# Casting loads on GpSimd for the weights and the first batches of an attention and gMLP kernel

## The chip, the cores and the metric

The kernel runs on one core of one Trainium2 chip. A core has five instruction queues that run side by side: TensorE (PE, matrix products; its weight loads are shown as PEld), VectorE (DVE), ScalarE (ACT), GpSimd (POOL) and SyncE (SP), which here only starts transfers. Sixteen DMA engines move the data between the memory of the chip (HBM) and the core's SBUF. Each queue works its own list strictly in order; semaphores tie the lists together.

The metric is the device time of one execution in microseconds (us). A run below is one timed execution; the profiled execution is another one.

## The reference

Sliding-window causal attention (window 64) over q, k, v of shape 8 batches x 8 heads x 576 positions x 64, all float32, then a gated MLP with a spatial product over the 576 positions.

```python
def _attn_ref(q, k, v):
    scores = (1 / np.sqrt(D)) * np.matmul(q, k.transpose(0, 1, 3, 2))
    rel = pos[:, None] - pos[None, :]
    scores = np.where((rel >= 0) & (rel < 64), scores, -1e9)
    attn = np.exp(scores - np.max(scores, axis=-1, keepdims=True))
    attn = attn / (np.sum(attn, axis=-1, keepdims=True) + 1e-09)
    return np.matmul(attn, v)

def _moe_ref(x, w_in, w_spatial, b_spatial, w_out):      # x: 8 x 576 x 512
    h = np.maximum(x @ w_in, 0.0)                        # w_in: 512 x 1024
    u, v = h[..., :512], h[..., 512:]
    v_n = (v - mean(v)) / np.sqrt(var(v) + 1e-06)
    v_s = np.einsum('ts,bsd->btd', w_spatial, v_n) + b_spatial[None, :, None]
    return (u * v_s) @ w_out                             # w_out: 512 x 512
```

## The kernel before

All products run in float16; inputs and output are float32. The work is cut into named steps. A step is one or a few instructions of one engine, and the string ORDER (line 18) lists all of them with their engine and the number of the buffer or PSUM bank that they take. The kernel walks that list and emits the steps, so each engine's queue is the list filtered for that engine; there is no loop that could reorder anything. `DQ` is SP's queue of transfers. `PH` is a TensorE step whose matmuls are issued as two halves of 64 columns of the weights.

The names, with batch b, half g of the heads (four heads each) and further digits:

- `D`: 27 warm-up steps of TensorE on a scratch tile (line 862), 25 with two matmuls of 512 columns, D25 and D26 with nine of 128.
- `ldk`, `ldq` (line 412): one transfer of 128 rows x 4608 B in float32 into a buffer of the tag `nat`; `ck`, `cq`: cast to float16 into `hqk` (helper `cp`, lines 290 to 300; on GpSimd in three pieces); `tk`, `tq` (line 419): 32 x 32 block transposes on VectorE.
- `ldv` (line 433): five transfers per b and g, 128 positions x 4 heads x 256 B each (the last one 64 positions), into `natv`; `cv`: casts into `hv`; `sl`, `su`, `s4`: copies between the partition halves into `hs`, the values shifted by 64 positions.
- `S` scores on TensorE (line 479, into a pair of PSUM banks), `E` exponential on ScalarE (486), `M` mask by a minimum on VectorE (489), `Z` row sums by a product with ones (502), `N` and `n` logarithm and negative exponential on ScalarE (529, 531) for the reciprocal, `P` the product with the values (514), `X` the product with the reciprocal on VectorE (522). `S_r` to `X_r` do the last 64 positions.
- `V` and `U` are the two halves of x @ w_in, `Vr` and `Ur` their ReLU on ScalarE (669, 763), `Vb`, `Va` the statistics on VectorE (671, 673), `L1`, `L2` the reciprocal root on ScalarE (716, 718), `A` the normalization (728), `G` the spatial product, `Ge` the gate (797), `O` the output product, `Oe` its copy, `st` the store.
- `ldwin`, `ldwsp`, `ldb`, `ldwo` load the weights in float32 into `nat` buffers; `cwin`, `cwsp`, `cb`, `cwo` cast them. `W` transposes w_spatial on TensorE (378), `We` copies it out of PSUM.

A batch's G steps need A of all five row groups and all We; its U and V steps need the cast w_in and X. Eight `nat` buffers are shared by q, k and the weights. Batches overlap: while the gMLP part of batch b runs, the attention part of b+1 and the loads of later ones are in flight.

The opening of the order before, as the engines see it: TensorE has ten D steps, then S0_0, six D, S0_r, and the first G step (G0_0) after V0, U0, W, Z1_10, Z1_11 and Z1_r. VectorE starts with the mask copies (lines 252 to 258), then ck0_0, tk0_0, cq0_0, tq0_0, tk0_1, cq0_1, tq0_1. GpSimd builds `keep`, the identity and the ones rows first (lines 244 to 264) and then has casts and half copies only. SP starts with ldb, ldk0_0, ldq0_0, ldk0_1, ldv0_00, ldq0_1.

Of the kernel before, what the change touches and what calls it, by code (L numbers as in the profile page):

```python
# [11 lines left out]
ALU = mybir.AluOpType  # L12
# [27 lines left out]
cq2_0:POOL:0 M1_10:DVE ldv1_10:DQ:3 Ur0_2:ACT:0 L10:ACT:0 ldv1_11:DQ ldv1_12:DQ ldv1_13:DQ L20:ACT  # L40
ldv1_14:DQ ldq2_1:DQ:5 ldv1_04:DQ ldk2_1:DQ:6 ldwo00:DQ:0 ldwo01:DQ Ur0_4:ACT:1 S1_r:PE:0:1
Z1_10:PE:3 U0_0:PE:1 ldwo10:DQ:7 ldwo11:DQ U0_1:PE:2 E1_r0:ACT:0 Ur0_3:ACT:2 E1_r1:ACT Ur0_0:ACT:3
N1_10:ACT:3 A0_0:DVE:0 A0_3:DVE:1 cwsp4:DVE Ur0_1:ACT:4 W1:PE:0 W3:PE:1 W2:PE:3 W0:PE:2 A0_1:DVE:2
A0_4:DVE M1_11:DVE We1:DVE M1_r:DVE n1_00:ACT We2:ACT We3:ACT A0_2:DVE:3 We0:DVE W4:PE:0 ldq3_0:DQ:1
ldk3_0:DQ:2 ldv2_00:DQ:1 ck2_0:POOL:2 We4:DVE D17:PE:3 Z1_11:PE:1 Z1_r:PE:2 G0_0:PH:3 G0_1:PH:0
tq2_0:DVE:2 n1_10:ACT N1_11:ACT:0 tk2_0:DVE:3 Ge0_0:DVE:0 cv1_00:ACT:2 n1_01:ACT sl1_00:POOL:2
n1_11:ACT su1_00:ACT N1_r:ACT:2 cv1_01:POOL Ge0_1:DVE:1 su1_01:DVE G0_3:PH:1 sl1_01:POOL
cv1_10:ACT:3 Ge0_3:DVE:2 cv1_11:DVE S2_0:PE:0:1 P1_01:PE:2 P1_00:PE:3 X1_00:DVE:2 G0_2:PH:0
sl1_10:POOL:3 ldv2_01:DQ ldv2_02:DQ su1_10:ACT sl1_11:ACT E2_01:ACT:3 n1_r:ACT su1_11:POOL
s41_1:POOL P1_10:PE:1 X1_01:DVE P1_11:PE:3 G0_4:PE:2 X1_10:DVE:3 X1_11:DVE U1_1:PH:1 cq2_1:POOL:3  # L50
E2_00:ACT:2 M2_01:DVE Ur1_1:ACT:5 Ge0_4:DVE:3 ck2_1:POOL:1 ldv2_03:DQ V1_2:PH:3 cwo01:POOL
cwo10:POOL cwo11:POOL Ge0_2:DVE:4 M2_00:DVE Z2_01:PE:2 s41_0:ACT Vr1_2:ACT:5 N2_01:ACT:1 U1_2:PH:1
Ur1_2:ACT:3 P1_r:PE:0 V1_1:PH:3 Vr1_1:ACT:6 cq3_0:POOL:0 Z2_00:PE:2 V1_3:PE:1 tq2_1:DVE:4
Vb1_2:DVE:5 V1_0:PE:3 ck3_0:POOL:2 tk2_1:DVE:5 S2_1:PE:1:0 X1_r:DVE:1 N2_00:ACT:4 Vr1_3:ACT:7
cwo00:ACT V1_4:PE:2 Vr1_0:ACT:1 U1_4:PH:1 O0_2:PH:0 Vb1_1:DVE:2 Vb1_3:DVE:3 Vb1_0:DVE:1 ldv2_10:DQ:0
E2_10:ACT:0 Vr1_4:ACT:2 ldv2_11:DQ Va1_3:DVE M2_10:DVE U1_3:PH:3 E2_11:ACT:1 cv2_00:POOL:0
Ur1_4:ACT:4 Va1_0:DVE Vb1_4:DVE:0 M2_11:DVE Va1_4:DVE Va1_2:DVE Va1_1:DVE Z2_10:PE:1 S2_r:PE:1:0
Oe0_2:ACT:0 Oe0_4:ACT:0 ldv2_12:DQ ldv2_13:DQ ldv2_14:DQ E2_r0:ACT:0 N2_10:ACT:5 ldk3_1:DQ:3
ldq3_1:DQ:4 ldk4_0:DQ:5 U1_0:PE:0 O0_3:PE:2 O0_0:PE:1 ldv3_10:DQ:3 ldv2_04:DQ tq3_0:DVE:7 E2_r1:ACT
L11:ACT:1 Ur1_0:ACT:2 Ur1_3:ACT:1 L21:ACT ldv3_11:DQ O0_1:PE:0 M2_r:DVE tk3_0:DVE:8 S3_0:PE:1:0  # L60
n2_00:ACT Oe0_3:ACT Oe0_0:ACT:1 A1_0:DVE:4 A1_1:DVE:5 A1_2:DVE:6 A1_3:DVE:7 A1_4:DVE sl2_00:ACT:0
Oe0_1:ACT Z2_r:PE:3 Z2_11:PE:2 N2_11:ACT:3 su2_00:DVE cv2_10:DVE:1 sl2_10:POOL:1 N2_r:ACT:0
ldv3_12:DQ st0_4:DQ ldv3_13:DQ G1_3:PH:1 G1_4:PH:0 P2_00:PE:2 P2_01:PE:3 s42_1:POOL su2_10:POOL
# [137 lines left out]
def kernel(  # L201
# [57 lines left out]
    NSB = 2  # L259
    mv_t = [cpool.tile([128, 5, 2], f32, name=f"mv{i}") for i in range(NSB)]  # L260
    vn4_t = [cpool.tile([65, 512], f16, name=f"vn4_{i}") for i in range(NSB)]
    for i in range(NSB):
        nc.vector.memset(mv_t[i][:], 1.0)
        nc.gpsimd.memset(vn4_t[i][64:65, :], 1.0)
# [37 lines left out]
    def cost(n, a=True, d=True, p=True, d1=False):  # L302
# [8 lines left out]
        return out  # L311

    WIN, WSP, WOUT = {}, [], []

    def win_steps(key):
# [600 lines left out]
```

## Time and profile before

| what | us |
|---|---|
| median of three runs | 196.23 |
| lowest and highest run | 195.93, 197.76 |
| span of the profiled execution | 193.6 |
| PE busy in the span | 184.9 |
| DVE busy | 163.7 |
| ACT busy | 157.1 |
| POOL busy | 87.4 |

The span runs from the first to the last instruction of the profiled execution; what lies around it (start and end of the program) isn't in it. For the profiled execution only its span is given; the median of the runs is 2.6 us longer than that. Busy time of PE counts overlapping matmuls once, and the warm-up steps too. The page's other figures that matter: DMA queues moved 42.73 MB at a mean of 221 GB/s, 50421 packets, 39377 of them under 512 B (the pieces of v). All transfers but three small groups start on SP's queue, none on GpSimd's.

In the rows that follow, a row of the timeline is start, duration, engine, line, operation, output <- input, count, and in brackets the idle time before it with what ended it.

### The profile page before, as it was taken

How to read it: one execution, taken by the hardware profiler on the slowest of the kernel's cores; microseconds unless marked ns; L12 is line 12 of the kernel's file. 1: busy time of each engine (PE TensorE's matmuls, PEld its weight loads, DVE VectorE, ACT ScalarE, POOL GpSimd, SP SyncE). 2: the span in 40 equal slices, each digit the busy share in tenths (PEclk: the TensorE clock that was granted, in tenths of full speed). 3: DMA queues.
4: the chain of work that ended last, by engine and by line, in shares of the span. 5: the costliest groups of instructions: out<-in, count | busy, mean ns of one | idle time of the engine just before them, and what ended most of it. 6: DMA issues, size and time to landing. Idle time of an engine off the chain costs nothing.

```text
span 193.6 us, 7606 instructions
## 1 busy us (share of the span) xinstructions
PE 184.9 (95%) x3218; PEld 107.0 (55%) x3218; DVE 163.7 (85%) x304; ACT 157.1 (81%) x282; POOL 87.4 (45%) x161
## 2 busy tenths in 40 slices
PE   7798998999999999999999999999999999999991
PEld 2352534556556664656665656565756565665560
DVE  4899899999999999998999999998996967468331
ACT  2269998998999999899979999999999875706430
POOL 4027775849932986701956577615641520000000
PEclk9999999999999999999999999999999999999999
DMA  5999999899989997619987999669958000600445
GB/s 177 373 316 290 391 355 333 168 275 373 242 205 332 261 335 179 149 38 289 367 230 184 310 310 282 196 177 218 306 125 266 22 3 0 224 30 0 135 166 191
DMA packets 50421, 42.73 MB, mean 221 GB/s; under 512 B 39377, under 2 KB 39761, under 8 KB 50386
## 3 DMA queue, kind: packets, MB, share of 16 engines
q1 hardware_dynamic: 50162, 42.04, 73.3%
q8 instruction: 25, 0.41, 0.9%
q10 hardware_dynamic: 224, 0.20, 0.3%
q14 instruction: 10, 0.08, 0.1%
HBM read 32.79 MB, written 9.44 MB: 218 GB/s over the span
## 4 chain that ended last, share of the span: by engine, by line
PE 70%; DVE 13%; ACT 9%; DMA 3%; issue 2%; SPq 1%
PE bank L617 50%; PE bank L614 4%; PE pair L479 4%; PE bank L514 3%; DMA nk<-in_k_dram 3%; PE bank L502 3%; ACT e L486 3%; DVE qT L419 2%; PE bank L702 2%; DVE e L489 2%; DVE kT L419 2%; DVE st L671 2%; DVE g L797 1%; DVE x L522 1%; ACT lz L529 1%
## 5 line engine op out<-in xcount | busy, mean ns | idle before, releaser
L617 PE MATMUL bank<-wspT,vn 128*64 128x512 f16 (+3 forms) x530 | 39.1, 296 | 0.0
L486 ACT ACTIVATE e<-pair 128x1024 f16<-128x1024 f32 x32 | 32.0, 1030 | 1.6 <-PE pair L479 1.4
L797 DVE TENSOR_TENSOR g<-bank,ru 128x512 f16<-128x512 f32 (+1 forms) x36 | 23.3, 654 | 9.4 <-PE bank L617 7.0
L647 ACT COPY ob<-bank 128x512 f32<-128x512 f32 (+1 forms) x38 | 21.9, 591 | 9.7 <-PE bank L617 8.4
L669 ACT ACTIVATE vs<-bank 128x512 f16<-128x512 f32 (+1 forms) x40 | 23.8, 602 | 7.1 <-PE bank L705 5.6
L617 PE MATMUL bank<-x,win 128*64 128x512 f16 (+2 forms) x304 | 29.1, 327 | 0.0
L617 PEld LDWEIGHTS <-vn 128*64 128x64 f16 (+1 forms) x530 | 20.8, 111 | 13.2 <-issue 0.2
L671 DVE BATCH_NORM_STATS2 st<-vs 128x6 f32<-128x512 f16 (+1 forms) x40 | 26.0, 670 | 2.3 <-ACT vs L669 2.2
L298 POOL COPY hs<-hv 64x512 f16<-64x512 f16 (+1 forms) x36 | 20.1, 585 | 16.3 <-ACT hv L292 8.4
L617 PE MATMUL bank<-win,x 128*64 128x512 f16 x216 | 27.0, 379 | 0.0
L617 PE MATMUL bank<-wout,g 128*64 128x512 f16 (+1 forms) x208 | 24.7, 371 | 0.0
L522 DVE TENSOR_TENSOR x<-bank,lz 128x512 f16<-128x512 f32 x32 | 21.2, 684 | 3.5 <-PE bank L514 2.2
L489 DVE TENSOR_TENSOR e<-e,mask 128x1024 f16<-128x1024 f16 x32 | 23.0, 725 | 0.5 <-ACT e L486 0.4
L763 ACT ACTIVATE ru<-bank 128x512 f32<-128x512 f32 (+1 forms) x38 | 21.6, 584 | 1.5 <-PE bank L617 0.8
L295 POOL CAST hk<-nk 128x384 f16<-128x384 f32 x36 | 19.4, 574 | 7.1 <-DMA nk<-in_k_dram 6.7
L529 ACT ACTIVATE lz<-bank 128x512 f32<-128x512 f32 x32 | 19.0, 599 | 1.9 <-PE bank L502 1.6
L298 POOL CAST hv<-nv 128x512 f16<-128x512 f32 x18 | 11.7, 661 | 18.8 <-DMA nv<-in_v_dram 18.7
L419 DVE STREAM_TRANSPOSE kT<-hk 128x576 f32<-128x576 f32 x16 | 19.9, 1241 | 0.2 <-ACT hk L292 0.2
L419 DVE STREAM_TRANSPOSE qT<-hq 128x576 f32<-128x576 f32 x16 | 19.8, 1237 | 0.2
L531 ACT ACTIVATE lz<-lz 128x512 f32<-128x512 f32 x32 | 19.6, 642 | 0.0
L295 POOL CAST hq<-nq 128x384 f16<-128x384 f32 x27 | 14.9, 588 | 10.3 <-DMA nq<-in_q_dram 7.8
L617 PEld LDWEIGHTS <-win 128*64 128x64 f16 x304 | 14.4, 110 | 9.2
(91 smaller groups left out, 298.9 us busy)
## 6 DMA issues: line engine op xcount, KB each, us to landing
nk<-in_k_dram SPq DMA_DIRECT2D x16, 576.0 KB, 6.6
nq<-in_q_dram SPq DMA_DIRECT2D x16, 576.0 KB, 6.1
nv<-in_v_dram SPq DMA_DIRECT2D x64, 128.0 KB, 5.9
out_dram<-ob SPq DMA_DIRECT2D x14, 512.0 KB, 5.8
wi<-in_moe_w_in_dram SPq DMA_DIRECT2D x8, 256.0 KB, 5.8
ws<-in_moe_w_spatial_dram SPq DMA_DIRECT2D x4, 288.0 KB, 7.6
nv<-in_v_dram SPq DMA_DIRECT2D x16, 64.0 KB, 4.5
wo<-in_moe_w_out_dram SPq DMA_DIRECT2D x4, 256.0 KB, 7.2
```

The source lines that it names most:

```text
L295: nc.gpsimd.tensor_copy(o[:, n:n + 384], i[:, n:n + 384])
L298: nc.gpsimd.tensor_copy(o[:, lo:hi, :, :], i[:, lo:hi, :, :])
L419: d = add(f"t{name}{b}_{g}", ("DVE", 1.09), key, lambda e: nc.vector.transpose(qt.t[:, :].rearrange("p (i j) -> p j i", j=18), h.t[:, :].b ...
L486: ex = add(f"E{b}_{g}{u}", ("ACT", 0.91), key, lambda e, u=u: nc.scalar.activation(e2[u].t[:, :, :], sc[u].t[:, :, :], AF.Exp, bias=0.0, s ...
L489: mins.append(add(f"M{b}_{g}{u}", ("DVE", 0.65), key, lambda e, u=u: nc.vector.tensor_tensor(e2[u].t[:, :, :], e2[u].t[:, :, :], mask[:, : ...
L522: lambda e, u=u, ob=ob, lz=lz: nc.vector.tensor_tensor(x.t[:, u, :], ob.t[:, :], lz.t[:, :], ALU.mult),
L617: nc.tensor.matmul(o[c:c + 64, :], w[:, c:c + 64], x, start=start, stop=stop)
L647: lambda e: (nc.vector.tensor_copy if last else nc.scalar.copy)(view(), m.t[rows, 0:n]),
L669: rl = add(f"Vr{b}_{j}", ("ACT", 0.49), key, lambda e: nc.scalar.activation(vs.t[0:jn, :], m.t[0:jn, :], AF.Relu), deps=[pv], acq=[vs], us ...
L671: s1 = add(f"Vb{b}_{j}", ("DVE", 0.6), key + 0.02, lambda e: nc.vector.bn_stats(st6.t[0:jn, 0:6], vs.t[0:jn, :]), deps=[rl], acq=[st6], us ...
L763: lambda e, m=m, ru=ru, n=n: nc.scalar.activation(ru.t[:, 0:n], m.t[:, 0:n], AF.Relu), deps=[pu], acq=[ru], uses=[m])))
L797: nc.vector.tensor_tensor(g.t[:, 0:n], m.t[:, 0:n], ru.t[:, 0:n], ALU.mult)
```

## The change

Weights, q, k and v of batches 0 and 1, and q and k of batch 2 are now loaded by transfers that GpSimd starts and that turn float32 into float16 on the way. Their casts on VectorE, ScalarE and GpSimd are gone. The destinations are the same `nat` buffers (seen as float16), `hv` for v, and the weight tiles themselves, which become one tile each so that one transfer fills four row groups. w_spatial goes to a `nat` buffer and its last 64 rows to `ob4`. `keep`, the mask copies and the constants become steps of the order (`keep`, `mask`, `consts`), behind the first transfers. A step `hold` on GpSimd reads the last such q or k buffer and writes one element of the buffer of q of batch 3; the load ldq3_0, now the first of SP's queue, depends on it. From batch 2's v on, the loads are as before. The order is written anew; the opening is shown to the first G step.

```diff
 ORDER = """
...
+ldk0_0:POOL:0 ldk0_1:POOL:1 ldq0_0:POOL:2 keep:POOL mask:DVE D24:PE:0 D5:PE:1 D21:PE:2 D18:PE:3
+ldq0_1:POOL:3 ldv0_00:POOL:0 ldq1_0:POOL:4 ldv0_04:POOL ldv0_01:POOL consts:POOL D2:PE:0
+ldv0_10:POOL:1 ldv0_14:POOL ldv0_11:POOL D14:PE:1 D19:PE:2 D10:PE:3 D3:PE:0 ldk1_0:POOL:5 D1:PE:1
+D22:PE:2 D15:PE:3 ldwin1:POOL D6:PE:0 D0:PE:1 tk0_0:DVE:0 D26:PE:2 tq0_0:DVE:1 S0_0:PE:0:1
+E0_01:ACT:0 ldwsp4:POOL:0 ldk1_1:POOL:6 ldq1_1:POOL:7 tk0_1:DVE:2 D23:PE:3 ldwsp0:POOL:0
+ldwin0:POOL tq0_1:DVE:3 E0_00:ACT:1 S0_r:PE:1:0 D8:PE:0 M0_00:DVE D16:PE:1 ldb:POOL ldv1_10:POOL:2
+ldv1_11:POOL E0_r0:ACT:0 sl0_00:ACT:0 su0_00:DVE s40_0:DVE E0_r1:ACT S0_1:PE:1:0 M0_r:DVE
+E0_10:ACT:2 Z0_r:PE:2 N0_r:ACT:0 M0_01:DVE Z0_00:PE:3 D7:PE:0 N0_00:ACT:1 tq1_0:DVE:4 Z0_01:PE:1
+D4:PE:0 N0_01:ACT:2 n0_01:ACT ldq2_0:POOL:2 ldk2_0:POOL:1 M0_10:DVE sl0_01:DVE su0_01:DVE D12:PE:2
+D20:PE:3 D11:PE:0 ldv1_00:POOL:3 P0_00:PE:1 D25:PE:2 ldv1_01:POOL sl1_10:POOL:1 ldq2_1:POOL:3
+ldk2_1:POOL:4 ldwo:POOL su1_11:POOL su1_10:POOL sl0_10:DVE:2 s40_1:DVE su0_10:DVE sl0_11:DVE
+su0_11:DVE E0_11:ACT:3 M0_11:DVE n0_00:ACT X0_00:DVE:0 Z0_10:PE:3 Z0_11:PE:0 N0_10:ACT:3
+sl1_11:POOL n0_10:ACT N0_11:ACT:4 n0_r:ACT n0_11:ACT tk1_0:DVE:5 D13:PE:2 P0_01:PE:3 P0_10:PE:1
+X0_10:DVE:1 P0_r:PE:2 X0_r:DVE:0 S1_0:PE:1:0 X0_01:DVE P0_11:PE:0 X0_11:DVE E1_00:ACT:1 M1_00:DVE
+E1_01:ACT:0 M1_01:DVE V0_4:PE:1 Vr0_4:ACT:0 Vb0_4:DVE:0 V0_3:PE:2 Z1_00:PE:3 Vr0_3:ACT:1
+N1_00:ACT:5 sl1_00:POOL:3 su1_00:POOL V0_1:PH:0 Vr0_1:ACT:2 tk1_1:DVE:6 Z1_01:PE:1 tq1_1:DVE:7
+V0_2:PE:2 sl1_01:POOL ldv1_04:POOL Vr0_2:ACT:3 Vb0_2:DVE:1 Va0_2:DVE Vb0_1:DVE:2 hold:POOL:5
+V0_0:PE:3 Vr0_0:ACT:4 Va0_4:DVE ldv1_14:POOL Va0_1:DVE ldq3_0:DQ ldv2_10:DQ:0 ldv2_13:DQ
+ldv2_00:DQ:1 ldv2_01:DQ ldk3_0:DQ:6 ldv2_02:DQ ldv2_03:DQ ldv2_11:DQ ldv2_12:DQ S1_1:PE:1:0
+E1_10:ACT:2 s41_0:POOL D9:PE:0 E1_11:ACT:3 W2:PE:2 W3:PE:3 We2:DVE D17:PE:0 Vb0_0:DVE:3 W4:PE:2
+W0:PE:0 Va0_0:DVE M1_10:DVE Vb0_3:DVE:4 Va0_3:DVE We4:ACT N1_01:ACT:1 S1_r:PE:1:0 We3:DVE L10:ACT:0
+L20:ACT A0_3:DVE:0 A0_1:DVE:1 We0:ACT W1:PE:2 U0_0:PE:1 U0_2:PE:3 We1:ACT n1_01:ACT A0_4:DVE
+U0_4:PE:0 U0_3:PE:2 Ur0_0:ACT:0 Ur0_2:ACT:1 Ur0_4:ACT:2 cq3_0:POOL:0 ck3_0:POOL:1 Ur0_3:ACT:3
+E1_r0:ACT:0 M1_11:DVE A0_0:DVE:2 A0_2:DVE:3 G0_4:PH:1 Ge0_4:DVE:0 Z1_10:PE:3 N1_10:ACT:3 E1_r1:ACT
...
-    w_in_sb = [cpool.tile([128, 1024], f16, name=f"win{r}") for r in range(4)]
-    w_out_sb = [cpool.tile([128, 512], f16, name=f"wout{r}") for r in range(4)]
+    w_in_all = cpool.tile([128, 4, 1024], f16, name="win")
+    w_in_sb = [w_in_all[:, r, :] for r in range(4)]
+    w_out_all = cpool.tile([128, 4, 512], f16, name="wout")
+    w_out_sb = [w_out_all[:, r, :] for r in range(4)]
...
+    kept = add("keep", ("POOL", 0.7), -2.0, emit_keep)
+    masked = add("mask", ("DVE", 2.0), -2.0, emit_mask, deps=[kept])
+    ids = add("consts", ("POOL", 1.8), -2.0, emit_consts)
...
     def win_steps(key):
         for half in (1, 0):
             cs = slice(512 * half, 512 * half + 512)
...
+            ld = add(f"ldwin{half}", ("POOL", 0.85), key + 0.01 * (1 - half),
+                     lambda e, cs=cs: nc.gpsimd.dma_start(
+                         w_in_all[:, :, cs], moe_w_in[:, cs].rearrange("(r p) f -> p r f", r=4)))
...
+        nat = [
+            add("ldwsp0", ("POOL", 0.85), key, lambda e: nc.gpsimd.dma_start(
+                wsb.t[:, :].bitcast(f16).rearrange("p (t s) -> p t s", t=4),
+                moe_w_spatial[0:512, :].rearrange("(t p) s -> p t s", t=4)), acq=[wsb]),
+            add("ldwsp4", ("POOL", 0.55), key + 0.001, lambda e: nc.gpsimd.dma_start(
+                wsl.t.bitcast(f16)[0:64, 0:576], moe_w_spatial[512:576, :]), acq=[wsl])]
...
         def one(name, src, key):
+            if b <= 2:
+                h = buf("nat", f"h{name}{b}_{g}")
+                c = add(f"ld{name}{b}_{g}", ("POOL", 0.55), key, lambda e: nc.gpsimd.dma_start(
+                    h.t.bitcast(f16)[:, 0:1152], src[b, 4 * g:4 * g + 4, :, :].rearrange("h (i j) d -> (h i) (j d)", j=18)),
+                    acq=[h])
+                HELD[:] = [h, c]
+                return turned(name, h, c, key)
+            hold = None
             n = buf("nat", f"n{name}{b}_{g}")
+            if (b, g, name) == (3, 0, "q"):
+                held = HELD[0]
+                hold = add("hold", ("POOL", 0.1), key, lambda e: nc.gpsimd.tensor_copy(
+                    n.t[0:1, 0:1], held.t[0:1, 0:1]), deps=[HELD[1]], acq=[n], uses=[held])
...
+        if early:
...
+                ld = add(f"ldv{b}_{g}{n}", ("POOL", 0.5 + 0.36 * w), key + 0.002 + 0.0001 * n,
+                         lambda e, lo=lo, hi=hi: [nc.gpsimd.dma_start(
+                             hv.t[:, c, :, :],
+                             v[b, 4 * g:4 * g + 4, 128 * c:128 * c + 128, :].transpose([1, 0, 2]))
+                             for c in range(lo, hi)],
+                         deps=done[:1], acq=[hv] if n == 0 else [], uses=[hv] if n else [])
```

In the new names ldv0_00 is two transfers (positions 0 to 255 of the first four heads), ldv0_01 the next two, ldv0_04 the last 64 positions; ldwin1 holds the columns of w_in for V, ldwin0 those for U. The numbers beside the engines are costs that the planner of the order used; the kernel does not read them.

428 lines of the change are left out of this document (191 added, 237 removed).

## The prediction

> **What bounds the kernel now.** I read the chain that ended last first, then stretches of it, then the timeline of the opening. The chain (start us, us, what) says who decides when:
>
> ```profile
> 2.10 6.08 DMA nk<-in_k_dram
> 11.27 1.26 DVE qT L419
> 19.08 0.60 ACT lz L529
> 28.64 1.15 DVE kT L419
> 33.81 1.83 PE bank L614 x8
> 35.65 2.23 PE bank L378 x25
> 38.86 3.25 PE bank L617 x30
> 68.38 0.22 PE bank L502 x2
> 68.59 1.73 PE bank L617 x16
> 189.57 0.37 ACT ob L835
> ```
>
> Up to 33.8 it goes through a transfer, VectorE and ScalarE; from there almost all of it is TensorE. The windows (stretch, length, busy PE, PEld, DVE, ACT, POOL, granted clock, DMA share, GB/s) agree:
>
> ```profile
> 5.00:35.00 30.00, 27.03 (x458) 12.96 (x457) 28.07 (x44) 23.28 (x42) 16.04 (x25) 1.00 1.09 339
> 35.00:50.00 15.00, 15.00 (x254) 8.98 (x253) 14.57 (x25) 13.78 (x25) 11.78 (x20) 1.00 0.90 282
> 50.00:160.00 110.00, 109.62 (x2127) 66.42 (x2126) 101.93 (x185) 104.44 (x187) 57.26 (x106) 1.00 0.77 216
> ```
>
> From 35 to 160 TensorE is idle for 0.4 us, at full clock. Before 35 its busy time is largely the 27 warm-up steps D, which both kernels hold; VectorE is the full engine (28.07 of 30) and the DMA engines are full (1.09, 339 GB/s). So a change can gain only by bringing TensorE's useful work forward in the opening, and each microsecond gained there reaches the end, if nothing later opens a gap.
>
> **The change, part by part.** Durations below are starts to starts of neighbours where engines pipeline. The opening, row by row:
>
> ```profile
> 1.21 0.38 SPq L412 DMA_DIRECT2D nk<-in_k_dram  x1
> 4.01 1.12 SPq L433 DMA_DIRECT2D nv<-in_v_dram  x2
> 1.27 6.87 PE L862 MATMUL bank<-scratch 128*128 128x512 f16 x20 [1.27 <-DVE scratch L237]
> 9.26 0.67 PE L479 MATMUL pair<-qT,kT 32*128 32x128 f16 x56 [1.12 <-DVE qT L419]
> 9.86 2.83 PE L862 MATMUL bank<-scratch 128*128 128x512 f16 x19
> 8.20 1.15 ACT L292 CAST hk<-nk 128x1152 f16<-128x1152 f32 x1 [6.11 <-DMA nk<-in_k_dram]
> 10.00 1.94 ACT L486 ACTIVATE e<-pair 128x1024 f16<-128x1024 f32 x2 [0.65 <-PE pair L479]
> 12.62 0.30 PE L553 MATMUL pair<-qT,kT 32*128 32x64 f16 x16
> 12.99 0.66 ACT L563 ACTIVATE er<-pair 128x256 f16<-128x256 f32 x2 [1.05 <-PE pair L553]
> 18.65 0.40 ACT L292 COPY hs<-hv 64x256 f16<-64x256 f16 x1
> 6.06 1.26 DVE L419 STREAM_TRANSPOSE kT<-hk 128x576 f32<-128x576 f32 x1
> 7.16 0.75 DVE L300 CAST hq<-nq 128x1152 f16<-128x1152 f32 x1
> 13.53 0.29 DVE L300 COPY hs<-hv 64x512 f16<-64x512 f16 x1
> 13.83 0.69 DVE L489 TENSOR_TENSOR e<-e,mask 128x1024 f16<-128x1024 f16 x1
> 14.44 1.17 DVE L300 CAST hk<-nk 128x1152 f16<-128x1152 f32 x1
> 22.67 1.29 DVE L522 TENSOR_TENSOR x<-bank,lz 128x512 f16<-128x512 f32 x2 [0.18 <-PE bank L514]
> 29.63 1.22 DVE L671 BATCH_NORM_STATS2 st<-vs 128x6 f32<-128x512 f16 x2
> 31.68 0.31 DVE L673 BATCH_NORM_AGGREGATE mv<-st 64x2 f32<-64x6 f32 x3
> 33.48 0.73 DVE L728 TENSOR_SCALAR vn<-vs,mv,ln 128x512 f16<-128x512 f16 x2
> 37.53 0.82 DVE L300 COPY wspT<-bank 128x576 f16<-128x576 f16 x2
> ```
>
> *First scores.* S0_0 stands behind 10 D steps now (20 matmuls, end 8.14) and waits for tq0_0 until 9.26. In the new order 14 D steps of 512 columns and D26 stand ahead of it: 8 more large and 9 small matmuls. The x19 row holds 10 large and 9 small in 2.83; less two large at 0.22 that is 2.4, so S0_0 starts at 10.5, 1.2 later than now. Its loads: ldk0_0, ldk0_1, ldq0_0 are three times 128 x 4608 B, 1.77 MB. Now the third such load lands at 8.20; at 339 GB/s 1.77 MB take 5.2, which leaves 3.0 us of start. By the same arithmetic q0_0 lands at 8.2 in the new kernel, tq0_0 ends at 9.5, one microsecond inside the D cover. The mask copies moved behind `keep` run before 6 and are covered too; without cover they cost about 2 us.
>
> *The start of VectorE's dense stretch.* From S0_0 (10.5 to 11.2): two E (1.94), S0_r (0.30), two E0_r with sl0_00 between (0.66 + 0.40) and some lag: 14.5, where M0_r starts.
>
> *Casts taken off VectorE.* ck0_0, cq0_0, cq0_1, ck1_0, cq1_1 and cwsp4 go; seven half copies sl0, su0, s4 come. From M0_r to A0_2 the new VectorE queue holds: 8 M at 0.61 (13.83 to 14.44) = 4.9; 4 transposes at 1.10 (6.06 to 7.16) = 4.4; 7 copies at 0.30 (13.53 to 13.83) = 2.1; 4 X at 0.60 (1.29 for two) and the half as wide X0_r 0.35 = 2.75; 5 Vb at 0.57 = 2.85; 5 Va at 0.10 = 0.5; We2, We3 at 0.41 = 0.8; 5 A at 0.33 = 1.65. Together 19.95, end at 34.45.
>
> *TensorE by the same walk.* tq1_1, reached after 12.3 of that sum, ends at 28.0. Then S1_1 (0.67), D9, W2, W3, D17, W4, W0, S1_r, W1 (five W in 2.23, D 0.43, S1_r 0.30) end at 32.1; U0_0, U0_2, U0_3 at 0.87 (1.73 for two such steps) and U0_4 as half a step end at 35.15. That is later than VectorE's 34.45, so G0_4 starts at 35.15. The kernel before starts G0_0 at 38.86. But it has then done U0_1 (0.87), Z1_10, Z1_11 (0.22 each) and the shorter Z1_r (0.1) besides: 1.4. Gain: 38.86 - 35.15 - 1.4 = 2.3 us. ScalarE between S0_0 and L20 holds 6 E at 0.97 and some 20 steps of 0.60 or less, under 18 us in 22; it is cover, not bound.
>
> *Casts off ScalarE and GpSimd* (cwin, cwsp, cwo, cv, ck, cq of batches 0 to 2): nothing, since TensorE is full from 35 on and hides them.
>
> *Transfers: bytes.* The byte count read is the same; what arrives when follows the GpSimd order. Up to ldv0_11 4.13 MB, ldwin1 5.77, ldq1_1 7.09, ldwsp0 8.27, ldwin0 9.32. With 3.0 + bytes/339 GB/s they land at 15.2, 20.0, 23.9, 27.4, 30.5; the walk needs them at 19.0 (sl0_11), 22.9 (V0_4), 26.8 (tq1_1), 29.1 (W2), 32.1 (U0_0). Margins are 1.6 to 3.8 us. No row shows a casting transfer. From below: writing half the bytes could be faster, which gains nothing as VectorE binds. From above: any slower rate; I take 339, the row of the same sources.
>
> *Transfers: issue.* Each casting load is issued on GpSimd, also unseen. Nearest row below: SP's 0.38 for q, k, 0.56 for a v piece. Add the 0.15 of GpSimd's smallest instruction (next fence): 0.53 and 0.71. From above: GpSimd work stretched beside VectorE, as here:
>
> ```profile
> 0.81 0.15 POOL L244 MEMSET keep<- 128x64 f16 x1 [0.29 <-POOLq L902]
> 1.52 0.20 POOL masks.py:197 MEMSET id<- 128x128 f16 x1
> 1.61 0.18 DVE L252 COPY mask<-keep 128x64 f16<-128x64 f16 x1 [0.32 <-POOL keep L247]
> 2.14 1.03 POOL L264 MEMSET vn<- 1x512 f16 x2
> 15.06 1.02 POOL L300 COPY hs<-hv 64x512 f16<-64x512 f16 x1
> 19.63 0.61 POOL L300 COPY hs<-hv 64x512 f16<-64x512 f16 x1
> ```
>
> The same copy takes 0.61 or 1.02, so 0.41 more. I take the lower price, since it is nearest in kind: ldv0_11 is the 15th transfer, 5 x 0.53 + 10 x 0.71 + `keep` 0.8 (0.81 to 1.61) + `consts` 1.65 (1.52 to 3.17) + 0.8 of start = 13.0; ldwin1 14.2, ldwin0 about 17.5. Bytes, not issue, then set the landings.
>
> [...]
>
> *Waits added.* sl1_10 waits on GpSimd for ldv1_10 (about 32), and ldq2_1, ldk2_1, ldwo are queued behind it; tq2_1 is wanted beyond 44. `hold` waits for k2_1 (12.73 MB, 40.6) and the whole SP queue stands behind it, batch 2's v first; v2 then lands by about 51, and P2_00 comes some 23 us of TensorE steps after G0_4, at 58. ldv1_14, cq3_0, ck3_0 and cv2_00 stand behind it on GpSimd, inside the same cover.
>
> *Sum.* Span 193.6 - 2.3 = 191.3. The median of the runs is 2.6 above the span, so 196.23 - 2.3 = 193.9.
>
> **The rivals.**
> *Slow issue (slower).* If each transfer takes 0.41 more, ldv0_11 is issued at 19.2 rather than 13.0 and lands 2.1 to 3.7 later, 2.3 to 3.9 past its need; VectorE's queue stands behind sl0_11. The time is 196.2 to 197.8, say 197.2. It decides from about 0.4 us more per transfer. For it: the 1.02 row, and some 25 us of issue in the first 35. Against it: every row of SP's unhindered issue is below 0.6.
> *Slow casting (slower).* At 250 GB/s ldwin0 lands at 40.3, 8.2 late: 202. It decides below 297 GB/s, where ldwin0 costs the whole 2.3. For it: margins of 1.6 us, and v rows of 256 B that become 128 B. Against it: only half the bytes are written.
> *A gap behind the opening (no change).* TensorE has no idle time after 35 to lose, so any stall that the new order opens there, with VectorE at 14.57 of 15, is paid in full: 195 to 196.2. For it: VectorE is just as dense afterwards. Against it: five casts fewer.
>
> **How the numbers follow.** Forecast 0.60, slow issue 0.15, slow casting 0.10, a gap 0.15. One per cent is 1.96 us, about what a measurement here can tell from no change. The forecast's own range is 191.8 to 195: 0.48 faster, 0.12 within. Slow issue 0.12 slower, 0.03 within; slow casting 0.08 and 0.02; the gap 0.12 within, 0.03 slower. Together 0.48, 0.29, 0.23. The range reaches 191.8 (VectorE's end binds and the margins hold) to 198.5 (slow issue in full); beyond are mainly slow casting and the worst of slow issue.
>
> **What would show it.** Right: S0_0 at 10.5, VectorE without waits on a transfer from 14.5, G0_4 near 35, and the chain on TensorE after it. Wrong: VectorE or TensorE waiting for a DMA of hv, win or kT before 35 (issue, if the DMA share is low then; casting, if it is full at fewer GB/s), transfer instructions on GpSimd over 1 us, or TensorE idle between 35 and 60.

## The result and the profile after

| kernel | median us | runs | ratio to the kernel before, 95% interval |
|---|---|---|---|
| before | 196.12 | 20 | 1 |
| changed | 197.41 | 20 | 1.0056 [1.0038, 1.0073] |

The change makes the kernel slower by about half a per cent: a little, but the interval excludes both no change and the forecast gain. Ratios here and below leave out disturbed runs, medians don't. The span of the profiled execution went from 193.6 to 195.3 us. Beside the later experiments the spans of 112 runs of the kernel before are on record: their median is 194.35 us, that of 18 runs of the changed kernel 195.2, and a run is 1.7 us longer than its own span, not 2.6. So the profile of before shows an execution some 0.7 us quicker than usual, and a comparison with it makes the loss look larger by about that.

The same three windows of the changed kernel as the prediction shows of before (stretch, length, busy PE, PEld, DVE, ACT, POOL, granted clock, DMA share, GB/s):

```profile
5.00:35.00 30.00, 27.28 (x470) 14.51 (x469) 26.35 (x49) 20.60 (x35) 22.15 (x36) 1.00 1.40 180
35.00:50.00 15.00, 14.97 (x299) 9.88 (x301) 13.35 (x22) 11.71 (x24) 8.05 (x15) 1.00 1.05 208
50.00:160.00 110.00, 108.64 (x2024) 66.43 (x2009) 104.52 (x190) 100.28 (x180) 53.58 (x95) 1.00 0.73 211
```

VectorE has less to do up to 50 us, as meant. Behind 50 it has more, 104.52 against 101.93 us, and TensorE, which was idle for 0.4 us there, is now idle for 1.4. The opening, by the timeline:

```profile
8.70 1.26 DVE L406 STREAM_TRANSPOSE qT<-hq 128x576 f32<-128x576 f32 x1 [2.04 <-DMA hq<-in_q_dram]
10.02 0.67 PE L495 MATMUL pair<-qT,kT 32*128 32x128 f16 x56 [0.25 <-DVE qT L406]
27.09 1.23 DVE L406 STREAM_TRANSPOSE qT<-hq 128x576 f32<-128x576 f32 x1
34.90 0.72 DVE L744 TENSOR_SCALAR vn<-vs,mv,ln 128x512 f16<-128x512 f16 x2
35.77 0.82 PE L633 MATMUL bank<-wspT,vn 128*64 128x64 f16 x40
```

And the chain of waits (start us, us, what):

```profile
2.54 6.14 DMA hq<-in_q_dram
8.70 1.27 DVE qT L406
...
32.65 3.19 PE bank L630 x28
...
57.19 1.16 DVE qT L406
58.35 0.18 DVE vn L744
...
81.21 0.30 issue
...
111.43 0.49 issue
```

The chain starts with a load of q where it started with one of k, and passes to TensorE's long stretch at 32.65, a microsecond earlier than before (33.81). The rows at 57 and 58 and the two of "issue" come back below.

S0_0 starts at 10.02, tq1_1 ends at 28.32, G0_4 starts at 35.77: the opening runs close to the forecast. Three points of the list divide the rest. Up to G0_2 in the new order and G0_4 in the old one TensorE has done the same steps (this point, taken where the last matmul of that step starts, is called the joint below); the same holds at the start of G2_0; the third point is the end of the span.

| us | last matmul of G0_2 / G0_4 starts | start of G2_0 | span | first to second | second to end |
|---|---|---|---|---|---|
| before | 45.40 | 81.65 | 193.6 | 36.25 | 112.0 |
| changed | 43.89 | 81.64 | 195.3 | 37.75 | 113.7 |

So 1.5 us are gained by the joint at 44 us, 1.5 are lost up to 81 us, and 1.7 more behind. Where TensorE waits in the changed kernel (the PE rows with an idle time, and VectorE's rows ahead of the first):

```profile
57.11 1.24 DVE L406 STREAM_TRANSPOSE qT<-hq 128x576 f32<-128x576 f32 x1
58.20 0.32 DVE L744 TENSOR_SCALAR vn<-vs,mv,ln 128x512 f16<-128x512 f16 x1
58.57 1.88 PE L633 MATMUL bank<-wspT,vn 128*64 128x64 f16 x48 [0.53 <-DVE vn L744]
81.52 0.19 PE L530 MATMUL bank<-e,hv 128*64 128x64 f16 x1 [0.30 <-issue]
111.92 0.82 PE L630 MATMUL bank<-win,x 128*128 128x512 f16 x3 [0.49 <-issue]
```

The first wait is one of order: VectorE's list has tq3_0 (57.11) ahead of A1_1 (58.20), for which G1_4 and G1_3 wait; G1_3 is late by 0.7 us. At the other two TensorE stands between two matmuls of one step (P3_11, V4_1) and waits for nothing that the profile names ("issue"): the next step is late by 0.5 and 0.7 us against e12 below, the same kernel without these waits.

Behind G2_0 the loss is mostly not waiting. The windows from there to the end of the span, before and changed (columns as above):

```profile
81.65:193.65 112.00, 107.56 (x1871) 65.00 (x1869) 88.21 (x167) 88.10 (x157) 36.51 (x69) 1.00 0.60 176
81.64:195.30 113.66, 109.13 (x1791) 68.31 (x1790) 91.10 (x174) 85.68 (x154) 36.91 (x65) 1.00 0.53 157
```

TensorE's steps are the same in both windows, though fewer of them are split in halves in the new order, which saves some 80 matmuls. Yet it is busy for 1.6 us longer, at the same granted clock.

### The profile page after: what moved, and what is told of

Its sections match the earlier page's. It is cut to its first block, busy times and chain, and to the rows that moved or that the text cites. A ratio compares the mean times of both kernels' runs of the same rounds, so it can differ in the third digit from the quotient of the medians.

```text
span 195.3 us, 7423 instructions
## 1 busy us (share of the span) xinstructions
PE 185.9 (95%) x3165; PEld 111.6 (57%) x3165; DVE 162.7 (83%) x310; ACT 148.8 (76%) x268; POOL 87.5 (45%) x156
## 3 DMA queue, kind: packets, MB, share of 16 engines
q0 software_dynamic: 13488, 6.96, 27.2%
## 4 chain that ended last, share of the span: by engine, by line
PE 80%; DVE 9%; DMA 3%; ACT 3%; issue 2%; POOL 1%; DVEq 0%; POOLq 0%
PE bank L633 45%; PE bank L630 16%; PE pair L495 5%; PE bank L530 4%; DMA hq<-in_q_dram 3%; PE bank L518 3%; PE bank L718 3%; ACT e L502 2%; DVE qT L406 2%; DVE e L505 2%; DVE vn L744 1%; DVE kT L406 1%; DVE hs L284 1%; PE bank L362 1%; PE pair L569 1%
## 5 line engine op out<-in xcount | busy, mean ns | idle before, releaser
L633 PE MATMUL bank<-wspT,vn 128*64 128x512 f16 (+3 forms) x440 | 32.3, 296 | 0.6 <-DVE vn L744 0.5
L813 DVE TENSOR_TENSOR g<-bank,ru 128x512 f16<-128x512 f32 (+1 forms) x36 | 22.8, 652 | 8.4 <-PE bank L633 6.1
L633 PE MATMUL bank<-x,win 128*64 128x512 f16 (+2 forms) x304 | 26.0, 307 | 0.0
L633 PE MATMUL bank<-wout,g 128*64 128x512 f16 (+1 forms) x216 | 25.9, 372 | 0.0
L633 PEld LDWEIGHTS <-vn 128*64 128x64 f16 (+1 forms) x440 | 18.1, 110 | 11.9 <-DVE vn L744 1.4
L633 PE MATMUL bank<-win,x 128*64 128x512 f16 x192 | 23.9, 380 | 0.0
L282 POOL COPY hs<-hv 64x512 f16<-64x512 f16 (+1 forms) x26 | 15.0, 604 | 12.7 <-DVE hv L284 9.5
L279 POOL CAST hq<-nq 128x384 f16<-128x384 f32 x24 | 14.2, 630 | 9.6 <-DMA nq<-in_q_dram 8.9
L633 PEld LDWEIGHTS <-g 128*64 128x64 f16 x216 | 14.1, 110 | 7.3 <-issue 0.4
L279 POOL CAST hk<-nk 128x384 f16<-128x384 f32 x27 | 14.2, 560 | 8.5 <-DMA nk<-in_k_dram 4.6
```

The source lines that it names most:

```text
L279: nc.gpsimd.tensor_copy(o[:, n:n + 384], i[:, n:n + 384])
L633: nc.tensor.matmul(o[c:c + 64, :], w[:, c:c + 64], x, start=start, stop=stop)
L813: nc.vector.tensor_tensor(g.t[:, 0:n], m.t[:, 0:n], ru.t[:, 0:n], ALU.mult)
```

## The experiments

Theory A: the casting loads do what they should, and the order behind the opening, which was written anew as well, gives the gain back. Rival B: the casting loads themselves cost something later. Rival C: VectorE is so full that an earlier TensorE only meets its next wait. Theory D came up after the first four runs: TensorE runs out of instructions.

| label | median us | runs | ratio to before, 95% interval |
|---|---|---|---|
| e1_new_opening_old_rest | 201.89 | 6 | 1.0194 [1.0131, 1.0257] |
| e2_new_to_81_old_rest | 196.39 | 12 | 1.0000 [0.9962, 1.0038] |
| e3_old_opening_new_rest | 210.58 | 4 | 1.0717 [1.0666, 1.0769] |
| e4_two_gaps_mended | 196.81 | 12 | 1.0011 [0.9978, 1.0043] |
| e5_blocks_moved | 197.35 | 12 | 1.0056 [1.0021, 1.0091] |
| e6_before_blocks_moved | 200.91 | 6 | 1.0205 [1.0147, 1.0263] |
| e7_blocks_and_order | 197.42 | 12 | 1.0059 [1.0023, 1.0096] |
| e8_new_opening_old_rest_mended | 196.38 | 12 | 0.9997 [0.9965, 1.0030] |
| e9_graft_other_blocks | 195.28 | 12 | 0.9971 [0.9937, 1.0006] |
| e10_order_and_blocks | 199.18 | 6 | 1.0142 [1.0104, 1.0180] |
| e11_no_v_from_batch4 | 196.90 | 7 | 1.0068 [1.0041, 1.0094] |
| e12_changed_again | 198.44 | 1 | |
| e13_opening_kept | 195.97 | 12 | 0.9978 [0.9951, 1.0005] |
| e14_before_moved_no_v | 197.54 | 12 | 1.0075 [1.0047, 1.0104] |
| e15_graft_again | 196.40 | 12 | 0.9992 [0.9952, 1.0032] |
| e16_opening_kept_2 | 194.89 | 9 | 0.9925 [0.9896, 0.9955] |

### One opening with the other's rest: e1, e2, e3

The list is cut behind a step; what is left follows in the other kernel's order and on its engines, with buffers and banks dealt anew.

```diff
 ... G0_1:PH:0 Ge0_1:DVE:3 G0_2:PH:2
-tq2_1:DVE:1 tk2_1:DVE:2 sl2_00:POOL:0 Ge0_2:DVE:4 M2_00:DVE V1_0:PH:3
+n1_r:ACT s41_1:POOL U1_1:PH:0 Ur1_1:ACT:5 V1_2:PH:3 Ge0_2:DVE:4 M2_00:DVE
...
```

> The changed kernel up to and with its step G0_2 (every TensorE step up to there is the same set as in the kernel before up to its G0_4), and behind it the remaining steps in the order and on the engines of the kernel before. At this cut the changed trace is 1.5 us ahead (43.89 against 45.40 us). Theory A (the casting loads bring what they should, and the rest of the order, written anew too, gives it back): about 1.5 us faster than the kernel before, 194.6 us. Rival B (the casting loads themselves cost later: hold, the queue of SyncE, batch 2's v late): 196 us or more, with waits on a DMA behind 42 us. Rival C (VectorE is as dense in either order, so an earlier TensorE only runs into it): 195.5 to 196.2 us, with new gaps in the order of before.

> The changed kernel up to and with its step P3_11 (80.8 us), and behind it the remaining steps as in the kernel before. At the cut both traces stand at the same time (G2_0 at 81.64 and 81.65 us). Theory A: the new order loses 1.5 us between 43 and 81 us and 2.2 us behind 81, so this kernel is like the one before, 195.2 to 196.2 us, and about 1.5 us slower than the kernel with the old order from 43 us on. Rivals B and C: no difference between these two kernels, and both within 0.5 us of the kernel before or slower.

> The other way round: the opening of the kernel before, with its plain loads and casts, up to its G0_4 (45.40 us), and then the changed kernel's order. Six casts that the changed kernel doesn't have (q and k of batch 2, w_out) are put at the joint. From the joint to the end the changed trace takes 147.1 us, the one before 143.4. Theory A (the loss is the order's own): up to 3.7 us slower than the kernel before, 198 to 199.8 us. Rival C (the order stalls only because its TensorE is early): 196 to 197 us. Rival B (casting loads at fault): like the kernel before, 196.1 us.

e1 and e3 missed by far, through their joints. In e1 the copy s41_1, now on GpSimd, stood behind two casts whose loads were late:

```profile
52.32 0.28 PE L606 MATMUL bank<-er,hs 128*64 128x64 f16 x6 [3.43 <-POOL hs L277]
```

In e3, with the q and k buffers dealt anew, GpSimd waited 10.3 us for loads of q. Neither tells the theories apart. e2 came out as A said, equal to the kernel before; but B and C allow for that too.

### Two gaps mended: e4

```diff
-cq3_1:POOL:2 tq3_0:DVE:3 A1_1:DVE:7
+cq3_1:POOL:2 A1_1:DVE:7 tq3_0:DVE:3
...
-sl3_10:DVE:1 M3_r:DVE su3_10:DVE M3_10:DVE
+sl3_10:POOL:1 su3_10:POOL M3_r:DVE M3_10:DVE
```

> The changed kernel with two small edits of its order: A1_1 ahead of tq3_0 on VectorE (TensorE waits 0.53 us for that vn at 58.6 us, G1_3 is late by 0.75), and the copies sl3_10 and su3_10 from VectorE to GpSimd, which is idle then (0.77 us ahead of the A2 steps for which G2_0 waits, 0.6 late). Theory A: each gap is worth its size, 197.4 less 1.3 is 196.1 us. Rival C: what is gained is lost at the next VectorE wait, 197 us or more. Rival B: no change, 197.4 us.

196.81: by the ratios 0.9 us less than the changed kernel, of the 1.3 that A gave. G1_3 was no longer late, but at 82 us TensorE stood for longer than in the changed kernel (G2_0 late by 0.8 us instead of 0.5), although the A2 steps now ended at 80.92, well ahead. So VectorE wasn't what TensorE waited for there.

### Blocks of instructions: e5 to e8

The page lists a queue that carries no data:

```profile
q8 instruction: 24, 0.39, 0.8%
```

24 transfers of 16,384 B for the changed kernel's 6330 matmuls and weight loads, 25 for the 6436 of the kernel before: about one for each 256 of them. Theory D reads from this that each transfer brings TensorE the next 256, called a block here. At both "issue" waits TensorE stood at a multiple of 256 of them (plus 188; plus 186 to 190 at all the waits listed below), and a transfer had begun shortly before: 79.08 us for the wait that ended at 81.52, 109.30 for the one that ended at 111.92. The profile gives no other wait of TensorE's matmuls to "issue" in the changed kernel, and none in the kernel before. To move the block ends, dummy matmuls are split or merged.

```diff
-NWARM, NFILL, FILL = 27, 2, 9
+NWARM, NFILL, FILL = 27, 0, 9
```

> The changed kernel with the two dummy steps of nine 128-column matmuls (D25, D26) made like the other dummies, two of 512 columns each: 0.50 us becomes 0.43, and 28 TensorE instructions (matmul and weight load) fewer stand ahead of all that follows. Theory D: TensorE's instructions arrive in blocks of 256; the trace has a 16,384-byte instruction transfer per block, and where TensorE needs the block within about 2.4 us of that transfer's start, it stands still. In the changed trace this is so twice, at 81.0 (1.94 us from start to need) and at 111.05 (1.75 us), where TensorE waits 0.6 and 0.75 us for nothing else that the profile names; the shortest two blocks are run through in 3.74 and 4.20 us. Moved by 28 instructions the shortest block lasts 4.7 us, as in the kernel before (4.66), which has no such stop. Expected: both stops go, 197.4 less 1.3 is 196.1 us. Rival A (the stops are VectorE's, through the order): no change, 197.4. Rival C: gone there, but lost at the next VectorE wait, 197 us.

For e6, in the kernel before:

```diff
-            for c in range(2 if i < NWARM - NFILL else FILL):
-                n = 512 if i < NWARM - NFILL else 128
+            fine = i in (0, 6, 7, 8, 15, 16, 22, 23)
+            for c in range(8 if fine else 2 if i < NWARM - NFILL else FILL):
+                n = 128 if fine or i >= NWARM - NFILL else 512
```

> The counter-test on the kernel before: eight of its dummy steps have eight 128-column matmuls in place of two of 512 columns, the same 0.43 us each, and so 96 more TensorE instructions ahead of the rest. By its trace one block of 256 instructions is then run through in 1.93 us at 137 us (natural: 4.66 at the shortest), two more in 4.05 and 4.46. Theory D: a stop of 0.5 to 3 us opens near 138 us, 196.3 plus 1.5 is 197.8 us. Every other theory: no change, 196.3 us.

> e5 together with two edits of the order: A1_1 ahead of tq3_0 on VectorE (0.75 us at 59 us), and the copy sl7_00 from VectorE to GpSimd (S7_1 waits 0.30 us at 147.4 us for tq7_1 behind it). If the three causes are separate: 197.4 less 1.3, 0.7 and 0.3 is 195.1 us, faster than the kernel before by about 1.2. If they stand for the same slack (rival C): like e5.

> e1 again, with its joint mended: s41_1 back on ScalarE as in the changed kernel (on GpSimd it stood behind two casts, and P1_r waited 3.43 us for it), the banks behind the joint dealt to those longest free (U1_1 waited 0.64 us), and the 28 instructions fewer, which puts the old rest four instructions from where it lies in its blocks in the kernel before. Theory A and D together: the opening's 1.5 us are kept to the end, 196.4 less 1.5 is 194.9 us. Rival B (casting loads cost later): 196 us or more, with waits on a DMA behind 42 us.

The kernel before became slower by 2 per cent through a split of dummy matmuls alone. Its profile has three "issue" waits that it didn't have:

```profile
50.33 0.41 PE L617 MATMUL bank<-win,x 128*64 128x512 f16 x2 [1.33 <-issue]
124.09 0.19 PE L514 MATMUL bank<-e,hv 128*64 128x64 f16 x1 [0.82 <-issue]
145.01 0.19 PE L514 MATMUL bank<-e,hv 128*64 128x64 f16 x1 [1.20 <-issue]
```

One was expected, near 138. (Some 1.8 us of its loss lie ahead of the joint and are no such wait.) In e5 the stops at 81 and 111 were gone, but the lost time wasn't won back (its ratio is that of the changed kernel, 1.0056): its opening was 0.7 us later at the joint, and 113.6 us lay behind G2_0, against 113.7 in the changed kernel. In e7 and e8 a new stop came at 41.7 and 43.2 us, inside the scores S2_0, 112 instructions in 0.6 us; e8's:

```profile
43.16 0.23 PE L488 MATMUL pair<-qT,kT 32*128 32x64 f16 x6 [1.19 <-issue]
```

So the waits at the ends of blocks bear D out, but the length of the block in time doesn't decide alone: my own estimate from the traces (blocks above 4.6 us are safe) failed in e7, e8 and e10. All 14 waits at a block's end that made TensorE's next matmul 0.25 us or more late in the traces of this study, by the start of the block's transfer and the moment when TensorE went on (us):

```
changed  79.08  81.52 | 109.30 111.92     e8   40.81  43.16
e2      106.24 108.47                     e9  110.42 112.84
e4       79.91  82.10                     e10  65.90  68.43
e6       47.64  50.33 | 121.76 124.09 | 142.79 145.01
e7       39.37  41.72                     e14  46.35  48.79 | 139.09 141.71
e15     111.87 114.29
```

TensorE goes on 2.2 to 2.7 us behind the start, each time (two smaller waits, 0.12 us in e3 and 0.17 in e16, ended 2.9 and 3.5 us behind it). What varies is when the transfer starts. For all blocks entered behind 10 us in the 18 traces, counted from the first matmul of the block before (the one at a multiple of 256 plus 190), by the mean busy share of the DMA engines in the 2 us from there on:

```
DMA share   transfers   median delay us
below 0.3     103         -0.3 (ahead of that matmul)
0.3 to 0.9    113          0.3
above 0.9     227          2.2
```

### Order or loads: e9 to e12

e9 is e8 without the 28 instructions fewer; e10 moves e7's blocks the other way; e11 leaves out loads:

```diff
+            if b <= 3:
+                NV[g] = buf("natv", f"nv{b}_{g}")
-            nv = buf("natv", f"nv{b}_{g}")
+            nv = NV[g]
...
-                               lambda e, c=c, sn=sn: nc.sync.dma_start(
+                               lambda e, c=c, sn=sn: b <= 3 and nc.sync.dma_start(
```

> e8 without the shift of 28 instructions: new opening to G0_2, then the rest of the kernel before, joint mended, D25 and D26 as they were. e8 lost 1.37 us at 41.7 to 43.2 us, inside S2_0, where a block of 256 TensorE instructions ended and the next one's transfer had started only 1.0 us earlier (it resumed 2.35 us after that start). Put 28 instructions earlier, the boundary lies outside S2_0; by e8's trace the shortest block then lasts 4.5 us. Theory A and D: the opening's gain is kept, 196.0 less 1.2 is 194.8 us. If casting loads cost later (B): 196 us or more.

> The changed kernel with A1_1 ahead of tq3_0 and sl7_00 on GpSimd as in e7, and the blocks moved the other way: D12 and D13 have ten 128-column matmuls in place of two of 512 columns, 32 TensorE instructions more. By the changed trace the shortest block then lasts 4.5 us (105 us) and none below 5 lies near 40 us, where e7 stopped for 1.3 us. Theory D: no stop over 0.5 us; 197.4 less 0.7 (A1_1), 1.3 (the two stops) and 0.2 is 195.2 us. If the new rest itself is slower by small losses, as the lag behind 81 us in e7 suggests (3.4 us against 1.7 to 2.3 with the old rest): 196.2 us.

> The changed kernel without the loads of v of batches 4 to 7 (40 of SyncE's transfers, 4.7 MB); their casts read batch 3's v again, so those batches are computed from the wrong v, and all other work stays. It asks why the instruction transfers start late. Over nine traces their start lies 0.3 us (median) behind the entry of the block before where the DMA engines are below 0.3 busy, and 2.2 to 2.5 us where they are above 0.9. If data transfers hold them up (D): the stop at 111 us goes, the one at 81 us shrinks at most a little, 197.4 less 0.75 is 196.6 us, and the transfers behind 85 us start within 1 us. If not: 197.4 us and the same delays.

> The changed kernel itself, one more profile. Theory D: the waits for a block come again at the same instructions, multiples of 256 (the last matmul of P3_11 at 81 us, V4_1 at 111 us), but with other lengths, since the transfer starts at another moment; 0 to 1 us each. Theory A (order): G1_3 late by 0.7 us at 59 us again, as the same VectorE step stands ahead. 197.4 us, plus or minus 0.8.

e9 is faster than the changed kernel by 1.7 us (by the ratios) and at least equal to the kernel before, with the new opening in it (the same kernel again, e15, came out at 196.40, so its gain over the kernel before is not certain). Its profile, of one of the longer runs (198.13), shows a wait at the joint, through a load of v that GpSimd issues behind `hold`:

```profile
48.43 0.40 ACT L269 COPY hs<-hv 64x256 f16<-64x256 f16 x1 [4.60 <-DMA hv<-in_v_dram]
49.50 1.05 PE L626 MATMUL bank<-x,win 128*64 128x512 f16 x8 [2.80 <-ACT ru L772]
```

e10 missed by 4 us, the other way. TensorE waits for VectorE, which e4's edit brings about when VectorE is late (Ge1_4 behind tk3_0), and at a block's end; e10's timeline:

```profile
61.12 1.27 PE L626 MATMUL bank<-wspT,vn 128*64 128x512 f16 x10 [1.06 <-DVE g L806]
68.43 0.38 PE L623 MATMUL bank<-wspT,vn 65*128 65x512 f16 x1 [1.13 <-issue]
```

In e11 the DMA share from 85 to 160 us fell from 0.65 to 0.34 and neither stop is in its profile. The median, 196.90, is near the forecast 196.6, but beside the kernel before of the same time the kernel is no faster than the changed one (1.0068 against 1.0056): a stop that is gone doesn't show in the time. e12, a single run: no "issue" wait, and the wait of G1_4 absent as well, because VectorE had time. Its opening was late: tq0_0 waited 3.44 us for hq, S0_0 began at 11.40, the joint was passed at 46.46. So waits of 81 and 111 us aren't in every execution, nor is the gain of the opening.

### The opening kept: e13 to e16

```diff
-sl1_01:POOL ldv1_04:POOL ... hold:POOL:5 ... ldv1_14:POOL
+ldwo:POOL ldv1_04:POOL ldv1_14:POOL su1_11:POOL ... hold:POOL:5
```

e13 also puts s41_1 behind Ur1_2; e16 leaves it where e9 has it. e15 is e9's kernel, e14 is e6 without v of batches 4 to 7.

> e9 with the two transfers ldv1_04 and ldv1_14 issued right behind ldwo, ahead of the seven shifted copies and of hold, and s41_1 behind Ur1_2 on ScalarE. In e9's profile s41_1 waited 4.60 us for ldv1_14 (issued at 41.94, landed at 48.4) with Ur1_1 behind it, and TensorE 2.8 us for that. Of e9's twelve runs eight lay at 194.7 to 195.6 and four at 197.3 to 198.4. Theory A: the upper group goes, 195.0 us, 1.0 below the kernel before. If the upper group is the opening's own (the first casting loads landing late, as in e12, where S0_0 began at 11.40): the same two groups, median 195.3 or above.

> e6 (the kernel before with its blocks moved by 96 instructions, 200.9 us) without the loads of v of batches 4 to 7, whose casts read batch 2's and 3's v again. e6 stopped for 1.33 us at 50.3, 0.82 at 124.1 and 1.20 at 145.0, each time 2.2 to 2.7 us behind the start of the instruction transfer. If data transfers hold that up: the stops at 124 and 145 go or halve, that at 50 stays, 200.9 less 1.5 to 2.0 is 199 us. If the number of instructions alone decides: the same three stops, 200.9 us.

> e9's kernel once more, for the comparison on the same chip: 195.3 us, some of the runs near 197.5. In the profile either the wait of some 3 us at U1_2 (then the span is 196.4), or none (then 193 to 193.5).

> e13 with s41_1 back in its place behind n1_r on ScalarE: ldv1_14 landed by 45.2 us in e13's profile, and ScalarE has nothing to do from 44.2 to 46.05, so the copy (0.40 us) costs nothing there, and P1_r doesn't wait 1.08 us for it. Theory A (the opening's gain is real and reaches the end behind the old rest): 196.0 less 1.0 is 195.0 us, narrow like e13 (195.1 to 196.8 there), 0.5 to 0.6 per cent below the kernel before. Rival C (the gain is eaten at the next wait): 196 us.

In e13 no run is above 197 us any more (four of twelve in e9, six of twelve in e15), but its timeline shows what s41_1's new place costs:

```profile
49.07 0.28 PE L606 MATMUL bank<-er,hs 128*64 128x64 f16 x6 [1.08 <-ACT hs L269]
```

e16 takes that away and is the fastest kernel of the study, 1.66 us below the median before of the same runs (196.55; by the ratio 1.5). Its copy s41_1, in ScalarE's timeline, waits for nothing, where in e9 it waited 4.60 us:

```profile
43.45 0.40 ACT L269 COPY hs<-hv 64x256 f16<-64x256 f16 x1
```

Its window behind 50 us:

```profile
50.00:160.00 110.00, 109.48 (x2130) 66.75 (x2131) 98.97 (x182) 102.79 (x184) 55.87 (x102) 1.00 0.73 209
```

Its joint is passed at 43.97 us, as in the changed kernel (43.89); from there it takes 36.17 us to G2_0 and 112.3 to the end (span 192.5), where the changed kernel takes 37.75 and 113.7. Opening and loads are the same, apart from the two early loads of v. So A holds: the order behind the opening costs 2.6 us by the ratios (0.9925 against 1.0056; the two spans are 2.8 apart), and B is out as an explanation of them. e2 divides the loss: with the new order up to 81 us and the old one behind it has the ratio 1.0000, so the new order costs about 1.5 us up to there and 1.1 behind, each uncertain by some 0.9 by the intervals.

Up to G2_0 most of it is the two waits of the changed profile: e12, the same kernel without them, takes 36.50 us where the changed kernel takes 37.75 and the one before 36.25. Behind G2_0 it isn't a wait at a block's end. The seven profiles with the new rest in its own buffers (changed, e4, e5, e7, e10 to e12) took 113.0 to 113.9 us from there to the end, and six of them have no such stop in that stretch; in each, TensorE is busy for 108.9 to 109.4 us of it. The old rest took 112.0 to 112.6 in six profiles (before, e1, e2, e8, e13, e16) and 112.5 to 114.8 in four with longer stops at a block's end or fewer loads (e6, e9, e14, e15), and in all ten TensorE is busy for 107.6 to 108.1. What lengthens TensorE's own work in the new order stays open: in e12 TensorE is never idle for more than 0.2 us at a time behind G2_0, e11 shows the longer work without the late loads of v as well, and no run isolates it. Rival C isn't settled either. In the window from 50 to 160 us VectorE is busy for 98.97 us in e16 and 104.52 in the changed kernel, and a VectorE that is 95% busy may turn small delays into waits of TensorE; no run shows that by itself.

In e14 the stop at 124 us is gone, and the ones at 145 and 50 are 0.25 and 1.05 us (at 141.71 and 48.79 there). A window of e6, columns as above:

```profile
85.00:160.00 75.00, 72.64 (x1403) 44.31 (x1404) 66.64 (x120) 69.48 (x120) 37.57 (x66) 1.00 0.76 214
```

The same window of e14:

```profile
85.00:160.00 75.00, 74.32 (x1450) 45.42 (x1450) 67.83 (x122) 70.73 (x123) 36.00 (x62) 1.00 0.40 139
```

And the stop at 48.79 in TensorE's timeline of e14:

```profile
48.79 0.41 PE L621 MATMUL bank<-win,x 128*64 128x512 f16 x2 [1.05 <-issue]
```

The same order of TensorE's steps, about half the DMA share, 1.7 us more of busy TensorE in 75; ahead of 70 us, where the loads are the same, the stop stays. So behind 85 us, at a share of 0.40 in place of 0.76, the stops fell from 2.02 us to 0.25, as they should if data transfers hold up the instruction transfer; by what means they would, no run shows. By the ratios e14 is 2.5 us faster than e6; the three stops went from 3.35 us to 1.30.

## Why the prediction was wrong

The step that failed is the sum, "193.6 - 2.3": it carries the opening's gain to the end unpaid, and has no term for the new order behind the opening. The walk stops at G0_4, and the text costs nothing behind it but the added waits and the casts that went away. Yet the diff has a new ORDER to its last line: of the 209 neighbouring pairs of TensorE steps behind G0_4 in the old list only 39 are neighbours in the new one. The price of that order is what the table above shows: 1.5 us up to G2_0 and 1.7 behind (by the ratios of e16, e2 and the changed kernel about 1.5 and 1.1). With the old rest behind the new opening, e16, the gain of the joint, 1.4 us, does reach the end (1.5 by the ratio). The condition "if nothing later opens a gap" was too narrow as well: behind G2_0 the time went with hardly a gap, in a TensorE that was busy for longer.

- *First scores* and *the dense stretch of VectorE*: right. S0_0 10.02 for 10.5, tq1_1's end 28.32 for 28.0, VectorE without a wait on a transfer from 10 to 35 us. But the load of q that S0_0 waits for has no margin: in the profiles of this opening S0_0 lies between 9.46 and 11.40.
- *TensorE by the same walk*: the mechanism right, the size off. G0_4 came at 35.77 for 35.15, and G0_0 of before starts at 38.69, not at 38.86, which is the start of a piece of the chain; so the gain is 1.5 us, not 2.3, and 1.5 at the joint too; over ten profiles of this opening (changed, e1, e2, e4, e5, e10 to e13, e16), which pass the joint at 43.77 to 46.46 us, median 44.3, against 45.40, it runs from 1.6 to -1.1, median 1.1.
- *Transfers: issue*: right. A q or k costs GpSimd 0.54 to 0.68 us (0.53 foreseen), a larger one 0.7 to 0.9 (0.71). The stretching beside VectorE that the dearer price came from (0.61 to 1.02 us for one copy on GpSimd) isn't seen at the issues: of the two loads of w_in, the one at 17.28, beside VectorE's copies from 17.07 on, took 0.86 us, the one at 14.19, beside two of its mask steps, 0.81; ldb, at 18.02 beside the same copies, took 0.69.
- *Transfers: bytes*: right. The landings foreseen for 15.2, 20.0, 23.9, 27.4 and 30.5 us came at 16.2, 21.3, 24.5, 27.7 and 30.2, and no step of VectorE or TensorE in the opening but tq0_0 waited for a load.
- *Casts off ScalarE and GpSimd*, costed at nothing: no run contradicts it.
- *Waits added*: the load ldv1_14 behind `hold` was noted and taken as covered; behind the old rest it wasn't (e9, 2.80 us), in the changed kernel it was.
- The rivals: slow issue and slow casting didn't occur. "A gap behind the opening" did up to G2_0, for the reason given (no idle time of TensorE to lose, VectorE dense), but it was priced as a return of the gain at most, 195 to 196.2, and the new order took more, behind G2_0 without a gap.

## What to carry to other kernels

When a diff replaces a hand-written order, the prediction has to walk every stretch that the order covers, or at least to compare the load of the busiest engine in each; a gain counted at one point of the list holds only if what follows is the same. Idle time alone doesn't price an order: compare the busy time of TensorE for the same steps too. To find out which part of such a change pays, join one's opening to the other's rest at a point where both have done the same set of steps, and mend the joint before reading the time. A wait that the profile gives to nothing ("issue") at the same instruction again and again is worth a look at the instruction transfers.

## What the runs showed of the hardware

- At 14 waits at the end of a block of 256 matmuls and weight loads, the longest of 1.71 us (e15), TensorE went on 2.2 to 2.7 us behind the start of an instruction transfer. In the 18 traces these transfers started later where the DMA engines were busy (median 2.2 us behind the first matmul of the block before at a share above 0.9, 0.3 ahead of it below 0.3). Blocks with steps of many small matmuls (scores, values) were run through in 3.5 and 4.5 us ahead of the changed kernel's two stops, counted as in the table, and 96 more instructions in dummy steps made the kernel before 2 per cent slower.
- GpSimd's transfers wait for each other. In the changed kernel's trace its 38 casting loads share eight semaphores (99 to 106), and those from the ninth on wait, by themselves or through an instruction ahead of them, for the semaphore that the load before on the same one sets, so that at each issue eight at most are under way. In the opening this cost GpSimd the idle times of these rows and two shorter ones (0.36 and 0.29 us):

```profile
21.62 1.48 POOL L423 DMA_DIRECT2D hv<-in_v_dram  x2 [1.77 <-DMA win<-in_moe_w_in_dram]
28.22 0.54 POOL L385 DMA_DIRECT2D hk<-in_k_dram  x1 [2.64 <-DMA wsp<-in_moe_w_spatial_dram]
30.52 2.98 POOL L423 DMA_DIRECT2D hv<-in_v_dram  x4 [1.75 <-DMA win<-in_moe_w_in_dram]
```

- From 5 to 35 us the casting transfers gave a DMA share of 1.40 at 180 GB/s, where the plain loads gave 1.09 at 339. The 6.96 MB that the profile counts on the queue of GpSimd's transfers are half of the 13.9 MB that their shapes read in float32, so it is the bytes written that it counts there.
